# Folding the first batch of a spectral mixture-of-experts kernel: 4-KB loads, sums and differences before the transform, quartered matmuls

## The chip, the cores and the metric

The kernel runs on one core of one Trainium2 chip. The metric is the device time of one execution in microseconds; the time of a kernel is the median of its runs. The engines are TensorE (PE in the profile; PEld is its weight load), VectorE (DVE), ScalarE (ACT), GpSimd (POOL) and SyncE (SP), which here issues the transfers.

## The reference, cut to what matters

Eight batches of 3072 x 256 go through a real Fourier transform along the sequence, a complex 256 x 256 mix with bias and soft threshold, and the inverse transform; a soft mixture of experts and a gated block with layer norm follow.

```python
X = np.fft.rfft(x, axis=1)                       # x: 8 x 3072 x 256
Yr = Xr @ w_r - Xi @ w_i + b_r
Yi = Xr @ w_i + Xi @ w_r + b_i
Yr = np.sign(Yr) * np.maximum(np.abs(Yr) - 0.01, 0)      # Yi likewise
y = np.fft.irfft(Yr + 1j * Yi, n=3072, axis=1)
# soft MoE over the 24576 rows of y: softmax over rows, experts on 32 slots, softmax over slots
# then h = x @ w_in;  solu = h * softmax(h);  layer norm;  @ w_out
```

## The kernel before

The transform of 3072 points is split as 96 x 32. Stage 1 is a transform over the 96 rows that lie 32 apart (index n1), for each of the 32 offsets n2; stage 2 combines the 32. The result of stage 1 goes through a DRAM buffer `ad`, because the two stages need different axes on the partitions. `load_ap` reads `ad` back, `stage2` transforms, `mix` multiplies with the weights (each fp32 operand split into a high and a low part, so three products), and so on. Phase 1 does this for the 8 batches in 12 steps each; phase 2, from about 620 us on, does the expert and the gated block.

Stage 1 exists in two forms. For batches 1 to 7 (`load_x`, `xfold`, `xdiff`, `stage1`, `a_fold`) it is folded: rows n1 and n1 + 48 are added and subtracted first, by POOL, and the sums and differences go through two 48 x 48 transforms. A unit holds four n2: two in partitions 0 to 47, two in partitions 64 to 111. Its four matmuls use a constant `fold` of 128 x 128, each a quarter of the array with 48 rows and up to 64 columns, and it stores 48 partitions at a time. Units 8 to 63 are spread over the steps of the main loop by `s1_next`.

Batch 0 has a form of its own (`load_x0`, `stage1_first`, `a_out`): 16 pieces of two n2 each. A piece is loaded with 2-KB rows into 96 partitions, goes through one 96 x 96 matmul with the constant `dft` (the profile shows two instructions for one fp32 product), is copied from PSUM by ACT and stored to `ad` by SP. All 16 loads are issued first, into buffers of the pool `s_p`. Nothing else can be done before the first blocks of `ad` can be read, except the preparation of the mix weights (`weights`, on DVE).

Order is written out by hand. Each engine executes its instructions in program order. `after(n, f)` puts a step off by n ticks, and `tick()` runs what is due. SP issues all transfers in program order: a transfer that must wait holds up those behind it. Behind the 16 pieces come `load_ap(0,0,0)`, a part of the constant `d2_sb`, `fold`, `load_x(8)` (the first load of batch 1), `load_ap(0,0,1)`, the bias and `load_x(9)`, then the main loop. Pools `ap_p`, `xt_p`, `y_p`, `st_p` for the main loop are opened at the beginning of phase 1.

## Time and profile before

| | us |
|---|---|
| median of 3 runs | 1340.09 |
| lowest, highest | 1338.70, 1341.55 |
| the profiled execution | 1339.27 |
| its span | 1337.2 |

| engine | busy us | share of the span |
|---|---|---|
| PE | 1265.9 | 95% |
| PEld | 1113.8 | 83% |
| DVE | 1143.4 | 86% |
| POOL | 1020.3 | 76% |
| ACT | 987.7 | 74% |

The page has one profiled execution. Busy shares are averages over the whole span; the edit is at its beginning, so the views by stretch of time and the chain of waits are read in what follows. Times of rows count from the first instruction. In a row of the timeline stand start, duration, engine, line, operation, output<-input by the program's names, shape and count; a bracket at the end is the idle time before it and what ended it. Rows with a count above one are merged, and their duration is from the first start to the last end.

### The profile page before, as it was taken

How to read it: one execution, taken by the hardware profiler on the slowest of the kernel's cores; microseconds unless marked ns; L12 is line 12 of the kernel's file. 1: busy time of each engine (PE TensorE's matmuls, PEld its weight loads, DVE VectorE, ACT ScalarE, POOL GpSimd, SP SyncE). 2: the span in 40 equal slices, each digit the busy share in tenths (PEclk: the TensorE clock that was granted, in tenths of full speed). 3: DMA queues.
4: the chain of work that ended last, by engine and by line, in shares of the span. 5: the costliest groups of instructions: out<-in, count | busy, mean ns of one | idle time of the engine just before them, and what ended most of it. 6: DMA issues, size and time to landing. Idle time of an engine off the chain costs nothing.

```text
span 1337.2 us, 30847 instructions
## 1 busy us (share of the span) xinstructions
PE 1265.9 (95%) x10980; PEld 1113.8 (83%) x10980; DVE 1143.4 (86%) x1562; ACT 987.7 (74%) x1830; POOL 1020.3 (76%) x1116
## 2 busy tenths in 40 slices
PE   5989999999999999998599999999999999999998
PEld 2867878786867778875399999999999999999998
DVE  1868898887897979765898999999999999999993
ACT  3445556555555555544598999999999999999995
POOL 0868696877767674442299999998999989999996
PEclk8999999999999999999699999999999999999999
DMA  9987474654639273339567777777777777777763
GB/s 267 277 219 189 118 206 126 173 160 125 192 82 247 72 206 138 112 115 364 123 165 195 190 214 193 190 189 184 201 195 196 181 190 199 189 201 176 196 169 109
DMA packets 181337, 241.77 MB, mean 181 GB/s; under 512 B 21984, under 2 KB 137056, under 8 KB 181184
## 3 DMA queue, kind: packets, MB, share of 16 engines
q1 hardware_dynamic: 180736, 238.62, 66.3%
q8 instruction: 87, 1.43, 0.5%
q10 hardware_dynamic: 448, 1.18, 0.2%
q14 instruction: 66, 0.54, 0.1%
HBM read 92.00 MB, written 59.11 MB: 113 GB/s over the span
## 4 chain that ended last, share of the span: by engine, by line
PE 69%; DVE 10%; DMA 7%; POOL 5%; issue 4%; ACT 3%; SPq 2%; DVEq 0%; POOLq 0%; ACTq 0%
PE po L89 33%; PE pb L89 8%; PE pm L89 6%; PE xps L89 5%; PE hps L89 5%; PE s L89 4%; PE pa L89 3%; POOL ul L1177 2%; DMA xc<-in_x_dram 2%; DVE u L1082 2%; PE sps L92 2%; PE hps L92 1%; DVE st L1067 1%; DVE tb L1105 1%; DMA ad<-asb 1%
## 5 line engine op out<-in xcount | busy, mean ns | idle before, releaser
L1177 POOL TENSOR_TENSOR ul<-t,uh 128x512 fp32r<-128x512 f32 x338 | 433.4, 1299 | 37.5 <-ACT uh L1163 35.1
L89 PEld LDWEIGHTS po<-gw,uh 128*128 128x128 f32 x2736 | 350.5, 190 | 14.0
L89 PE MATMUL po<-gw,uh 128*128 128x256 f32 x2736 | 356.9, 282 | 0.0
L1067 DVE TENSOR_REDUCE st<-hps 128x1 f32<-128x1024 f32 x192 | 229.2, 1194 | 14.0 <-PE hps L89 13.9
L89 PE MATMUL po<-gw,ul 128*128 128x256 f32 x1620 | 230.8, 285 | 6.8 <-POOL ul L1177 6.6
L1082 DVE SCALAR_TENSOR_TENSOR u<-hps,e 128x1024 f32<-128x1024 f32 x192 | 232.2, 1209 | 0.5 <-ACT e L1074 0.3
L1074 ACT ACTIVATE e<-hps,st 128x1024 f32<-128x1024 f32 x192 | 215.5, 1123 | 16.8 <-DVE st L1067 16.7
L1187 ACT ACTIVATE sq<-u,st 128x1024 f32<-128x1024 f32 x192 | 223.0, 1161 | 0.3 <-DVE u L1082 0.3
L1105 DVE STREAM_TRANSPOSE tb<-u 128x1024 f32<-128x1024 f32 x169 | 210.5, 1246 | 7.0 <-DMA t<-tb 1.2
L89 PEld LDWEIGHTS po<-gw,ul 128*128 128x128 f32 x1620 | 207.5, 189 | 9.4 <-POOL ul L1177 8.4
L347 POOL TENSOR_TENSOR s<-yb,s 128x512 f32<-128x512 f32 x95 | 124.6, 1312 | 113.4 <-DVE s L346 109.8
L89 PEld LDWEIGHTS xps<-d_sb,apt 128*128 128x128 f32 x768 | 95.0, 194 | 59.7 <-issue 35.3
L1163 ACT ACTIVATE uh<-t 128x768 fp32r<-128x768 f32 x169 | 143.6, 850 | 0.9 <-DMA t<-tb 0.9
L89 PE MATMUL xps<-d_sb,apt 128*128 128x128 f32 x768 | 111.0, 288 | 13.1 <-DMA apt<-ad 10.2
L89 PE MATMUL hps<-gst,ct 128*128 128x512 f32 x338 | 107.7, 401 | 13.9 <-DVE u L1082 12.5
L250 ACT ACTIVATE asb<-s 128x1024 f32<-128x1024 f32 x56 | 57.6, 1029 | 82.9 <-PE s L89 71.4
L223 POOL TENSOR_TENSOR x<-xc 112x512 f32<-112x512 f32 x56 | 75.4, 1347 | 42.8 <-DMA xc<-in_x_dram 39.8
L307 POOL TENSOR_TENSOR sl<-xsum,sh 128x256 fp32r<-128x256 f32 x93 | 76.3, 821 | 37.1 <-ACT sh L306 36.9
L291 DVE TENSOR_TENSOR xsum<-xps,xi 128x256 f32<-128x256 f32 x96 | 39.9, 415 | 67.3 <-ACT xh L290 48.0
L1238 ACT ACTIVATE osb<-po,st 128x256 f32<-128x256 f32 x192 | 80.3, 476 | 11.4 <-PE po L89 11.4
L1164 POOL CAST uh<-t 128x256 fp32r<-128x256 f32 x169 | 68.4, 405 | 24.6 <-DMA t<-tb 24.6
L227 POOL TENSOR_TENSOR x<-xc 112x512 f32<-112x512 f32 x56 | 79.1, 1413 | 0.0
(210 smaller groups left out, 2373.5 us busy)
## 6 DMA issues: line engine op xcount, KB each, us to landing
t<-tb SPq DMA_DIRECT2D x676, 128.0 KB, 2.8
xc<-in_x_dram SPq DMA_DIRECT2D x128, 192.0 KB, 4.1
apt<-ad SPq DMA_DIRECT2D x96, 256.0 KB, 4.1
out_dram<-osb SPq DMA_DIRECT2D x47, 512.0 KB, 3.7
ad<-asb SPq DMA_DIRECT2D x112, 192.0 KB, 3.9
ct<-c_dram SPq DMA_DIRECT2D x96, 128.0 KB, 4.0
wt<-in_moe_w_dram SPq DMA_DIRECT2D x21, 512.0 KB, 9.6
ws<-in_moe_w_dram SPq DMA_DIRECT2D x22, 256.0 KB, 5.4
```

The costliest lines, as they stand in the source:

```text
L89: PE.matmul(out=out, lhsT=lhsT, rhs=rhs, start=start, stop=stop)
L227: POOL.tensor_tensor(out=z[0:112, 1], in0=t[:, 0], in1=t[:, 1], op=ALU.subtract)
L307: (POOL if (b, t) > (0, 2) else DVE).tensor_tensor(out=sl, in0=sm_, in1=sh.bitcast(F32), op=ALU.subtract)
L347: POOL.tensor_tensor(out=s, in0=y, in1=s, op=ALU.subtract)
L1067: DVE.tensor_reduce(out=st[:, 0, k:k + 1], in_=hps[i], op=ALU.min, axis=AX.X)
L1074: ACT.activation(out=e, in_=hps[i], func=AF.Exp, bias=st[:, 0, k:k + 1], scale=-1.0, accum_out=st[:, 1, k:k + 1])
L1082: DVE.scalar_tensor_tensor(out=u, in0=hps[i] if turned(i) else hps.pop(i), scalar=1.0, in1=et.pop(i), op0=ALU.mult, op1=ALU.mult, accum_ou ...
L1105: DVE.transpose(out=t, in_=ut[i])
L1163: ACT.activation(out=w[:, 0:HA], in_=v[:, 0:HA], func=AF.Copy)
L1177: POOL.tensor_tensor(out=ul[:, z, :].rearrange("p c (a j) -> p c a j", a=4), in0=v, in1=w.bitcast(F32), op=ALU.subtract)
L1187: ACT.activation(out=sq, in_=ut.pop(i), func=AF.Square, bias=st[:, 2, k:k + 1], scale=-float(DFF), accum_out=st[:, 3, k:k + 1])
L1238: ACT.activation(out=o[:, k], in_=pot.pop(i), func=AF.Copy, scale=stt[j][:, 4, k:k + 1])
```

## The change

Batch 0 is folded as well. Its 8 units take two buffers' halves each: four buffers `xt[v]` of 128 x 2 x 4 x 256, each loaded by two transfers with 4-KB rows into 48 partitions (64 to 111 first, then 0 to 47). Partitions 32 to 63 of the buffers are filled with zero before, by DVE and POOL in turn. The buffers lie in a pool `x0_p` that is closed before the pools of the main loop are opened, so these take its place. A unit's sum is made by DVE, its difference by DVE (even units) or POOL (odd units). The matmuls go to two PSUM banks, are copied by two ACT instructions, and two transfers store the unit. `fold` is loaded first of all, `dft` is gone. Six matmuls on `ones` (`warm(6)`) stand before the first unit and 34 behind `weights()`, ahead of stage 2 on TensorE. `load_x(8)` is issued before `load_ap(0,0,0)`. The order of the constants in the early loads is kept, at other unit numbers.

```diff
-        ap_p = right("ap_p", 2)
-        xt_p = right("xt_p", 2)
-        y_p = right("y_p", 2)
-        st_p = right("st_p", 5)
...
-        def load_x0(ch):
-            t = s_p.tile([96, 2, D], F32, name="xc0", tag="s")
-            SP.dma_start(out=t, in_=x[0].rearrange("(a n) d -> a n d", n=32)[:, 2 * ch:2 * ch + 2, :])
-            xt[ch] = t
+        x0_open = ExitStack()
+        x0_p = x0_open.enter_context(tc.tile_pool(name="x0_p", bufs=1, side="right"))
+
+        def load_x0(v, r):
+            rows = x[0].rearrange("(h a n) d -> a h n d", h=2, n=32)
+            SP.dma_start(out=xt[v][64 * r:64 * r + 48], in_=rows[:, :, 8 * v + 4 * r:8 * v + 4 * r + 4, :])
...
-        def stage1_first(ch):
-            if ch == 0:
+        def stage1_first(u):
+            v, w = divmod(u, 2)
+            if u == 0:
                 ad[0] = dram2.tile([32, 4, 24, D], F32, name="ad", tag="ad")
-            dst = s_p.tile([96, 2, D], F32, name="a0", tag="s")
-            after(LAG["a_out"], a_out, 0, 2 * ch, 2, dst)
-            pool, tag = ((ps1, "s1"), (pst, "sps"), (psm, "pm"))[ch % 3]
-            ps = pool.tile([96, 2, D], F32, name="s1", tag=tag)
-            mm(ps, dft, xt.pop(ch))
-            ACT.activation(out=dst, in_=ps, func=AF.Copy)
+            t = xt[v][0:112, :, w::2, :]
+            z = xc[u % 2] if u % 4 > 1 else wa_p.tile([128, 2, 2, D], F32, name="x1", tag="x1")
+            DVE.tensor_tensor(out=z[0:112, 0], in0=t[:, 0], in1=t[:, 1], op=ALU.add)
+            (POOL if w else DVE).tensor_tensor(out=z[0:112, 1], in0=t[:, 0], in1=t[:, 1], op=ALU.subtract)
...
+            unit(ps, z)
+            if u % 4 > 1:
+                dst = wa_p.tile([128, 2, 2, D], F32, name="a0", tag="asb")
+            else:
+                dst = sm_p.tile([128, 2, 2, D], F32, name="a0", tag=("sa", "sb", "sc")[u // 4 + u % 4])
+            for r in range(2):
+                ACT.activation(out=dst[:, r], in_=ps[r], func=AF.Copy)
+            after(LAG["a_out"], a_first, v, w, dst)
+
+        def a_first(v, w, t):
+            for c in range(2):
+                o = ad[0][:, 2 * c:2 * c + 2].rearrange("(v m w) k g d -> v w (k g) m d", v=4, w=2)
+                SP.dma_start(out=o[v, w], in_=t[64 * c:64 * c + 48])
+
+        def unit(ps, z):
+            for k in range(2):
+                for r in range(2):
+                    c = (k + r) % 2
+                    mm(ps[r][64 * c:64 * c + 64], fold[64 * r:64 * r + 48, 64 * c:64 * c + 64], z[64 * r:64 * r + 48, c])
...
-        for ch in range(16):
-            load_x0(ch)
+        def warm(n):
+            ps = psy.tile([128, 128], F32, name="warm", tag="pa")
+            for _ in range(n):
+                mm(ps, ones, ones)
+
+        load_const(fold, c_fold)
         POOL.memset(ones, 1.0)
+        for v in range(4):
+            xt[v] = x0_p.tile([128, 2, 4, D], F32, name=f"x0{v}")
+            (DVE, POOL)[v % 2].memset(xt[v][32:64], 0.0)
+        warm(6)
+        for v in range(4):
+            for r in (1, 0):
+                load_x0(v, r)
...
-        for pr in range(16):
-            stage1_first(pr)
...
+        for u in range(8):
+            stage1_first(u)
...
         tick()
+        x0_open.close()
+        ap_p = right("ap_p", 2)
...
         weights()
+        warm(34)
+        load_x(8)
         load_ap(0, 0, 0)
         load_const(d2_sb[:, 2:8, :], c_d2[:, 2:8, :])
-        load_const(fold, c_fold)
-        load_x(8)
         load_ap(0, 0, 1)
```

## Rows read from the trace of the kernel before

**Rows 1.** The page's first line.
```profile
span 1337.2 us, 30847 instructions
```

**Rows 2.** Chain of waits, first 60 us: start us, length us, what.
```profile
4.06 16.98 PE s L89 x32
21.06 0.60 ACT a L238
...
22.12 3.09 DMA ad<-a
...
25.33 2.83 DMA apt<-ad
...
28.30 2.15 PE xps L89 x8
...
32.63 2.05 PE xps L89 x8
34.68 3.43 PE pb L89 x18
```

**Rows 3.** Busy time by window: window, length, engines (instructions), PEclk, DMA share, GB/s.
```profile
3.50:13.00 9.50, 8.94 (x14) 3.26 (x15) 0.00 (x0) 3.49 (x6) 0.00 (x0) 1.00 1.04 263
...
25.00:28.00 3.00, 0.00 (x0) 0.00 (x0) 0.00 (x0) 0.00 (x0) 0.00 (x0) 0.50 0.53 145
...
29.90:31.30 1.40, 0.54 (x3) 0.24 (x2) 0.00 (x0) 0.83 (x2) 0.00 (x0) 0.50 1.09 231
...
100.00:120.00 20.00, 20.00 (x173) 15.62 (x172) 17.21 (x22) 11.19 (x22) 18.25 (x16) 1.00 0.71 190
606.00:612.00 6.00, 5.19 (x88) 4.55 (x88) 3.36 (x9) 3.23 (x7) 0.00 (x0) 1.00 1.03 414
```

**Rows 4.** First four and last load of batch 0, first `load_ap`: issue, landing.
```profile
L205 SPq DMA_DIRECT2D xc<-in_x_dram x4: 405/423/426, 1.2 to 2.6; - x4
...
DMA to landing us min/median/max: 2.7/3.5/4.3
...
L205 SPq DMA_DIRECT2D xc<-in_x_dram x1: 312/312/312, 10.0 to 10.0; - x1
...
DMA to landing us min/median/max: 5.3/5.3/5.3
...
L266 SPq DMA_DIRECT2D apt<-ad x2: 343/384/426, 25.3 to 25.7; - x2
...
DMA to landing us min/median/max: 2.8/3.1/3.4
```

**Rows 5.** Timeline of DVE and POOL in the first 45 us.
```profile
1.39 1.84 POOL L787 MEMSET xc<- 128x1024 f32 x2
19.89 0.68 DVE L792 TENSOR_TENSOR wk<-wc 128x512 f32<-128x512 f32 x1
33.02 0.43 DVE L307 TENSOR_TENSOR sl<-xsum,sh 128x256 fp32r<-128x256 f32 x1
39.38 1.29 POOL L227 TENSOR_TENSOR x<-xc 112x512 f32<-112x512 f32 x1
42.33 1.46 POOL L227 TENSOR_TENSOR x<-xc 112x512 f32<-112x512 f32 x1
42.58 1.49 DVE L307 TENSOR_TENSOR sl<-xsum,sh 128x256 fp32r<-128x256 f32 x1
```

**Rows 6.** Timeline of TensorE and its weight loads.
```profile
34.27 0.97 PEld L89 LDWEIGHTS pb<-wc_h,xh 128*128 128x128 f32 x4
38.52 0.98 PEld L89 LDWEIGHTS xps<-d_sb,apt 128*128 128x128 f32 x8
39.42 0.54 PEld L89 LDWEIGHTS pb<-wc_h,xh 128*128 128x128 f32 x4
41.72 1.09 PE L89 MATMUL s<-x,fold 48*64 48x512 f32 x8
...
611.68 1.52 PEld L89 LDWEIGHTS idle<-ones 128*128 128x128 f32 x12
```

More of the change, by code (lines that the diff above doesn't have):

```diff
@@ L245, in stage1 @@
             ps = ps1.tile([128, 2, 2, D], F32, name="s1", tag="s1")
-            for k in range(2):
-                for r in range(2):
-                    c = (k + r) % 2
-                    mm(ps[64 * c:64 * c + 64, r], fold[64 * r:64 * r + 48, 64 * c:64 * c + 64], z[64 * r:64 * r + 48, c])
+            unit([ps[:, 0], ps[:, 1]], z)
             ACT.activation(out=dst, in_=ps.rearrange("p r n d -> p (r n) d"), func=AF.Copy)
@@ L720, in sums, with load_const @@
                 DVE.tensor_scalar(out=mexp, in0=mexp, scalar1=srun, scalar2=None, op0=ALU.mult)
+        def load_const(o, i):
+            SP.dma_start(out=o, in_=i)
         dec_ops = []
@@ L785, in phase1 @@
         POOL.memset(zx, 0.0)
-        for t in xc:
-            POOL.memset(t, 0.0)
         def weights():
```

28 lines of the change are left out of this document (15 added, 13 removed).

## The prediction

> **What bounds the kernel now.** The span comes first [rows 1]: it is 1337.2 us, in an execution timed at 1339.27 us, so 2.1 us lie around it. The median of the three runs is 1340.09 us. I subtract changes in the stretch that the edit touches and quote the result against the median; the profiled execution is 0.8 us below it.
>
> Next I read the chain of waits for the first 60 us [rows 2], because the edit touches nothing later. The reader is to see a row of handovers with one engine at a time. TensorE runs 32 stage-1 matmuls without a break from 4.06 to 21.04. One ScalarE copy of 0.60 follows, then the last store of stage 1 (issued 22.12, 3.09 to landing), then the first load of the intermediate (issued 25.33, 2.83 to landing), and at 28.30 stage 2 begins. Whatever moves 25.33, and whatever runs faster between 28.30 and the steady state, moves the end.
>
> [...] And from 100 to 120 us TensorE is busy 20.00 of 20 us: from there a head start is carried along by the bound engine. A gain at 28 to 40 us should therefore reach the end nearly whole.
>
> **The change, part by part.**
>
> *Loads.* Sixteen loads of 192 KB (2-KB rows into 96 partitions) become eight of 384 KB (4-KB rows into 48 partitions, upper half first). The bytes stay 3.15 MB. Before, the first four loads are 786 KB, the last of them issued at 2.6 and landed 4.3 later [rows 4]: 6.8 us. The last load lands at 10.0 + 5.3 = 15.3. In between the queues are full at 263 GB/s [rows 3]. The first pair of new loads is these same 786 KB. What 4-KB rows into 48 partitions cost is not in the trace, so I bound it. The rows at 29.9 to 31.3 us cover mostly a load of x into 48 partitions: 231 GB/s. Contiguous 4-KB rows into 128 partitions at 606 to 612 us: 414 GB/s. I take the 263 of the same data in the same place and let the first pair land at 6.8, with bounds 5.4 (786 KB at 414 instead of 263 saves 1.1 us, and I allow 0.3 for the shorter backlog) and 7.5 (at 231 it costs 0.4, and the fills below may add).
>
> [...]
>
> *Zero fill.* The fills of partitions 32 to 63 precede the second load of each pair. POOL fills 1024 elements in 0.92 us [rows 5], so 2048 in 1.84; DVE has no such row, and four times its 0.68 for 512 elements, 2.7, bounds it from above. SP stands in front of them in order, with the later loads behind it; but the first load of each pair is issued before the fill is waited for and needs 1.5 us of the queues at 263 GB/s. That is the cover. At 2.7 about 0.7 us would show, once, in the landing of the first pair.
>
> *Sums and differences.* New on the path: per pair three DVE operations and one POOL operation on 112 x 512 elements. DVE's comparable one took 0.68 [rows 5], POOL's 1.29. They don't run side by side: the DVE subtraction of 128 x 256 took 0.43 alone at 33.02, and 1.49 at 42.58 with a POOL subtraction in 42.33 to 43.79, ending 0.3 after it. So I add them: 3 x 0.66 + 1.26 = 3.25 us for a pair (spacing instead of duration). Pairs of loads arrive every 2.8 us ((15.3 - 6.8) / 3), slightly faster, so this is a chain that never drains: four pairs from 6.8 end at 19.8. If nothing collided, it would end about 2 us after the last load: 17.3. Queued behind it on DVE is the preparation of the mix weights, whose second instruction started at 19.89 before; it moves by less than 1 us and the mix that waits for it begins above 30, so it costs nothing.
>
> *Matmuls.* A folded unit took 1.09 us at the upper level [rows 6], eight take 8.7; 32 full ones took 17. The new ones aren't continuous at first, and I expect the first two or three units at the lower rate (before, the first 14 matmuls took 0.64 us each, the 18 behind them 0.45 [rows 2, 3]). TensorE has room for that, 3.25 us a pair. The last unit ends 1.1 to 1.45 after the chain: about 21.1, against 21.04 before. The path through TensorE is not shorter; the arithmetic it loses had been paid by waiting anyway.
>
> *Copies and stores.* ScalarE now makes two copies of 0.6 for the last unit, 0.6 more than before, and the second of its two stores is issued 0.4 behind the first. The last landing becomes 21.1 + 1.2 + 0.4 + 3.0 = 25.7 against 25.21. The queues themselves would allow 25.1: after the last load of x the same stores and weights need 25.2 - 15.3 = 9.9 us in both. Copies of units 4, 6 and 7 reuse buffers whose stores may land just in time; at most 0.6 us. So the load of the intermediate starts at about 25.8, **0.45 us later than before**; bounds are -1.5 and +1.5.
>
> *Moved load of batch 1 and the fold constant.* load_x(8) now goes ahead of load_ap: two issues of 0.4 us on SP and 1.5 us on the queues, both inside the 3 us in which the last store is landing. Without that cover they would cost up to 1.5. Gone from behind load_ap are these 384 KB and the 64 KB of the fold constant: d2, the second intermediate block and the bias land earlier by up to 1.9 us. That is needed, since the next step wants them earlier.
>
> *Warm matmuls.* 34 pairs of 128 x 128. The same product elsewhere took 1.52 us for 12 [rows 6], 0.12 each, so 68 x 0.12 = 8.2 us: from 21.1 to 29.3. The intermediate lands at 28.6, its second half 1.0 later, as before (25.7 + 3.4 against 28.16 [rows 4]). So they end beside the landing, and cost about 0.2. What they bring: stage 2 and the first mix run at the upper level. At the lower one the first group of eight took 2.15 and the second 2.05 [rows 2]; the same eight at 38.52 give way to the next after 0.90 [rows 6]. Walked through, from the landing: first group done after 1.75 instead of 2.28 (the second half of the block lands only 1.0 behind), the second group starts at 3.94 instead of 4.47 (ScalarE and DVE between them unchanged), the mix follows 0.90 instead of 1.67 later, and its 24 matmuls take 0.117 each, as at 39.42, where the first dozen took about 0.21, as at 34.27. The next stage-2 group starts 7.65 after landing instead of 10.36: **2.7 us won**. DVE, next in line there, gets its inputs 2.8 earlier as well.
>
> **Sum:** 2.7 - 0.45 - 0.15 = 2.1 us. 1339.27 becomes 1337.2 in an execution like the profiled one, and the median 1340.09 becomes **1338.0 us**.
>
> **The rivals.**
>
> *Faster loads.* If 4-KB rows run near 414 GB/s, the first pair lands at 5.4 and the chain of sums ends at 18.4: 1.4 more won, 1336.6. If sums and differences collide less as well, up to 3 more: 1335. For it: the contiguous rows. Against: the same destination partitions held 263. I put it at 1336.0.
>
> [...] Loads into half of the partitions hold 231 GB/s throughout, and less where one half waits for the other. At 231 they need 13.6 us instead of 12, the last pair lands 1.7 later, the last sums end 0.45 later: 1338.5; 1 us more of it gives 1339.5, still no difference that shows. [...]
>
> *The warm matmuls come late or run at the lower level* (the slower end). They stand in TensorE's order ahead of stage 2. If the units, in pieces, don't raise the clock, eight of them take 2 x 1.09 us each from about 9.4, to 27, and 68 warm ones at twice 0.12 take 16: the end is 43, 14.5 us after 28.30, less the 2.7. If the clock rises 6 us into the warm ones, they end at 32.7, 4.4 after 28.30, and the kernel is 1.7 us slower: 1341.8, and up from there. It decides from an end of the warm matmuls at about 31 us. Against it: before, 6 us of matmuls in a row were enough to run at the upper rate.
>
> *It doesn't arrive.* The transfers behind 40 us may be too full to let through what TensorE has won, and the gain ends as waiting for data: 1340.
>
> **How the numbers follow.** Forecast 0.60 (1336.4 to 1339.6; 1338.0), faster loads 0.20, ports 0.08, late warm matmuls 0.09, not arriving 0.03. About 0.2%, 2.7 us, is what a measurement of this kernel can tell from no change, so the line is 1337.4. It cuts the forecast's own range, 0.22 on the faster side and 0.38 on the other. Faster: 0.22 + 0.19 = 0.41. Same: 0.38 + 0.01 + 0.07 + 0.03 = 0.49. Slower: 0.10. The range 1335.0 to 1341.0 leaves out the best of the fast loads and most of the late warm matmuls.
>
> **What would show it.** In the trace of the changed kernel: first pair landed near 6.8; DVE and POOL stretched against each other until 19.8; the last unit near 21; load_ap at 25.3 to 26.3; the warm matmuls ending within 1 us of its landing; a granted clock of 1.00 from 25 to 40 us, and the first mix's end 2 us earlier. The prediction fails if load_ap is issued before 24 or after 27, if the clock is 0.50 behind the units, or if the head start at 40 us isn't found at 100 us.

## The result and the profile after

The changed kernel takes 1347.43 us (1342.40 to 1349.64, six runs) against 1338.55 us of the kernel before in the same runs. By these medians it is slower by 8.9 us, a quotient of 1.0066; the ratio estimated from the runs, as in the table below, is 1.0087 with a 95% interval of 1.0061 to 1.0112. So it is slower, clear of noise; the forecast was 1338.0 us, with a range of 1335.0 to 1341.0. The profiled execution took 1349.3 us, and its span is 10.3 us longer than that of [rows 1]:

```profile
span 1347.5 us, 31080 instructions
```

The sums by window of the changed kernel, as [rows 3]: window, its length, busy time of PE, PEld, DVE, ACT and POOL, granted clock, DMA share, GB/s.

```profile
3.50:13.00 9.50, 3.69 (x12) 1.21 (x14) 4.57 (x4) 0.00 (x0) 3.39 (x5) 1.00 1.03 164
...
29.40:37.60 8.20, 8.20 (x69) 8.13 (x68) 1.49 (x5) 1.08 (x2) 0.00 (x0) 1.00 0.79 215
37.60:40.50 2.90, 1.40 (x10) 1.04 (x8) 0.00 (x0) 0.00 (x0) 1.26 (x1) 1.00 0.95 322
40.50:47.50 7.00, 4.70 (x23) 4.61 (x22) 3.56 (x13) 2.58 (x6) 0.00 (x0) 0.52 0.94 243
```

The first line is the finding. The DMA share is 1.03 against 1.04 before, so the queues are just as full, but they move 164 GB/s instead of 263. The last line is the second finding: behind the warm matmuls the clock falls after all, to 0.52 in the mean from 40.5 to 47.5 us.

A third is hidden by the column of the granted clock. It prints 1.00 also where the trace has no record of the clock yet: the first record, a rise to 1.00, stands at 10.1 us in the kernel before and at 30.5 us in the changed kernel. The matmuls themselves show the level ahead of it. The groups below are the folded matmuls of the changed kernel between 9.5 and 29.3 us, and the same form in the kernel before between 39.5 and 66 us (count, then busy time and mean ns of one):

```profile
L88 PE MATMUL s<-x,fold 48*64 48x512 f32 x32 | 10.7, 1071 | 5.8 <-DVE x L232 5.8
```
```profile
L89 PE MATMUL s<-x,fold 48*64 48x512 f32 x40 | 5.4, 615 | 0.0
```

The other 32 of the changed kernel took 1070. So all eight units ran at the lower level, and it rose only 1.2 us into the warm matmuls. In the kernel before, the 96 x 96 matmuls took 1069 ns each up to 10.1 us and 612 behind it.

Issues and landings of the changed kernel, as [rows 4]: the first two loads, the last two, and the first block read back.

```profile
L202 SPq DMA_DIRECT2D x<-in_x_dram x2: 315/363/411, 1.2 to 3.0; - x2
...
DMA to landing us min/median/max: 5.2/5.5/5.8
...
L202 SPq DMA_DIRECT2D x<-in_x_dram x2: 357/394/431, 5.5 to 6.0; - x2
...
DMA to landing us min/median/max: 15.5/16.3/17.1
...
L281 SPq DMA_DIRECT2D apt<-ad x2: 351/387/423, 35.8 to 36.2; - x2
...
DMA to landing us min/median/max: 2.9/3.3/3.6
```

The first pair has landed at 3.0 + 5.8 = 8.8 us, the last load at 6.0 + 17.1 = 23.1, where 6.8 and 15.3 were forecast. The eight landings are 2.4 us apart, and 384 KB in 2.4 us are 163 GB/s. load_ap is issued at 35.84 us, 10.5 us later than before.

The timeline of DVE and POOL, as [rows 5]; a bracket is the idle time before the row and what ended it.

```profile
8.96 0.69 DVE L232 TENSOR_TENSOR x<-x 112x512 f32<-112x512 f32 x1 [3.85 <-DMA x<-in_x_dram]
9.57 1.75 DVE L233 TENSOR_TENSOR x<-x 112x512 f32<-112x512 f32 x1
11.25 0.68 DVE L232 TENSOR_TENSOR x<-x 112x512 f32<-112x512 f32 x1
13.87 0.69 DVE L232 TENSOR_TENSOR xc<-x 112x512 f32<-112x512 f32 x1 [1.94 <-DMA x<-in_x_dram]
...
9.00 1.77 POOL L233 TENSOR_TENSOR x<-x 112x512 f32<-112x512 f32 x1 [3.83 <-DMA x<-in_x_dram]
```

A pair takes 2.97 us (8.96 to 11.93) and then DVE waits 1.94 for the next load: the loads set the pace, not the sums.

The timeline of ScalarE and SP behind the loads:

```profile
25.52 2.06 ACT L247 ACTIVATE a<-s 128x512 f32<-128x512 f32 x4 [4.37 <-DMA ad<-a]
...
21.05 7.82 SPq L253 DMA_DIRECT2D ad<-a  x8
...
30.45 2.56 SPq L253 DMA_DIRECT2D ad<-a  x4
...
35.84 0.83 SPq L281 DMA_DIRECT2D apt<-ad  x2
```

The copy at 25.52 has waited 4.37 us for a store that had to land out of the same buffer, behind the loads. SP is at eight stores for 7.82 us, its waits for their copies included.

The weight loads of TensorE, as [rows 6]:

```profile
29.33 8.20 PEld L88 LDWEIGHTS warm<-ones 128*128 128x128 f32 x68 [1.61 <-issue]
39.00 0.52 PEld L88 LDWEIGHTS xps<-d_sb,apt 128*128 128x128 f32 x4 [1.47 <-issue]
...
42.89 1.78 PEld L88 LDWEIGHTS xps<-d_sb,apt 128*128 128x128 f32 x8 [2.47 <-issue]
44.55 0.97 PEld L88 LDWEIGHTS pb<-wc_h,xh 128*128 128x128 f32 x4
...
48.74 0.98 PEld L88 LDWEIGHTS xps<-d_sb,apt 128*128 128x128 f32 x8
```

The warm matmuls take the 8.2 us that were forecast, but TensorE then waits 1.3 us in front of the first group of stage 2 and 2.3 us in front of the second, and the level falls at 40.7 us, as the second wait begins. The mix spends 0.97 us on four weight loads, as at 34.27 before, and the third group starts at 48.74, 10.2 us behind the 38.52 of before. So in these two executions the whole loss of 10.3 us is there at 35.84 us and is carried to the end.

It splits in two. The last load of x lands 7.7 us late (23.1 against 15.4). From there to the landing of the last store it takes 12.6 us (to 35.70) instead of 9.8 (15.38 to 25.21): 2.8 us more. Together they are the 10.5. The two are not independent, as a run with punctual loads will show. The experiments take these two, and the clock behind 28 us, one by one; no run changes the clock of the units alone, whose last matmul ends 3.1 us behind the last sum (26.27 to 29.41), where it is 1.4 us in e10 (20.48 to 21.87) with its last units at the upper level.

### The profile page after: what moved, and what is told of

Read it like the earlier page. It is cut to its first block, busy times and chain, and to the rows that moved or that the text cites. A ratio compares the mean times of both kernels' runs of the same rounds, so it can differ in the third digit from the quotient of the medians.

```text
span 1347.5 us, 31080 instructions
## 1 busy us (share of the span) xinstructions
PE 1279.9 (95%) x11092; PEld 1124.0 (83%) x11092; DVE 1165.2 (86%) x1576; ACT 986.1 (73%) x1830; POOL 1027.9 (76%) x1120
## 4 chain that ended last, share of the span: by engine, by line
PE 61%; POOL 11%; DVE 9%; issue 6%; DMA 5%; SPq 3%; ACT 2%; POOLq 0%; DVEq 0%; ACTq 0%
PE po L88 33%; PE pb L88 6%; PE hps L88 5%; PE pm L88 5%; PE xps L88 4%; DMA xc<-in_x_dram 3%; POOL ul L1204 3%; PE pa L88 2%; PE s L88 2%; POOL x L219 2%; PE hps L91 1%; POOL x L223 1%; SPq L1136 1%; PE sps L91 1%; POOL s L362 1%
## 5 line engine op out<-in xcount | busy, mean ns | idle before, releaser
L1101 ACT ACTIVATE e<-hps,st 128x1024 f32<-128x1024 f32 x192 | 215.0, 1120 | 17.1 <-DVE st L1094 17.1
L322 POOL TENSOR_TENSOR sl<-xsum,sh 128x256 fp32r<-128x256 f32 x93 | 76.1, 818 | 35.1 <-ACT sh L321 34.9
```

The costliest lines, as they stand in the source:

```text
L1101: ACT.activation(out=e, in_=hps[i], func=AF.Exp, bias=st[:, 0, k:k + 1], scale=-1.0, accum_out=st[:, 1, k:k + 1])
```

## The experiments

One table for the loads and stores; the columns are landing times in us from the traces. "Between" is the time from the last load of x to the last store of stage 1. The ratios are against the kernel before in runs beside each. The kernels e6, e7, e10, e11, e13, e17 and e18 time the stage and do not compute the transform: they load other rows, and e13, e17 and e18 also store other data.

| kernel | last load | last store | between | load_ap issued | ratio (95%) |
|---|---|---|---|---|---|
| before | 15.38 | 25.21 | 9.8 | 25.33 | 1 |
| changed | 23.11 | 35.70 | 12.6 | 35.84 | 1.0087 (1.0061 to 1.0112) |
| e3 before, 4-KB rows | 14.82 | 24.80 | 10.0 | 24.99 | 1.0016 (0.9998 to 1.0035) |
| e6 source flat | 21.60 | 34.37 | 12.8 | 34.51 | 1347.8 us, one run |
| e7 128 partitions | 15.45 | 30.84 | 15.4 | 30.98 | 1.0053 (1.0032 to 1.0073) |
| e2 2-KB rows | 20.04 | 32.76 | 12.7 | 32.90 | 1.0106 (1.0073 to 1.0138) |
| e8 halves in turn | 18.52 | 31.48 | 13.0 | 31.63 | 1.0068 (1.0046 to 1.0089) |
| e1 two queues | 23.23 | 39.28 | 16.1 | 39.42 | 1.0130 (1.0093 to 1.0166) |
| e10 = e7 + own buffers | 16.36 | 31.33 | 15.0 | 31.48 | 1.0059 (1.0037 to 1.0080) |
| e11 = e10 + two issuers | 15.55 | 29.28 | 13.7 | 29.43 | 1.0054 (1.0035 to 1.0073) |
| e13 = e10 + 96-part. stores | 15.58 | 28.97 | 13.4 | 29.12 | 1.0035 (1.0020 to 1.0051) |
| e17 = e13 + two issuers | 16.17 | 28.49 | 12.3 | 28.64 | 1.0042 (1.0025 to 1.0059) |
| e18 = e13 - sums | 16.49 | 27.94 | 11.5 | 28.09 | 1.0026 (1.0008 to 1.0044) |
| e14 before, half stores | 15.08 | 27.17 | 12.1 | 27.36 | 1.0009 (0.9993 to 1.0026) |
| e12 all together | 19.28 | 33.30 | 14.0 | 33.52 | 1.0103 (1.0079 to 1.0127) |

Each landing is read from one execution. Loads that are the same in e7, e10, e11, e13, e17 and e18 landed between 15.45 and 16.49, and "between" was 9.86 in e15 and 10.75 in e16, two kernels below whose stage 1 and order of transfers are the same. So differences under about 1 us in these columns show nothing. Nor does load_ap give the time one to one: e2 has it 2.9 us earlier than the changed kernel and is no faster, and e11, with load_ap 4.1 us later than before, loses 6.5 us in the medians. These runs don't show where the rest is lost.

### What makes the loads slow

The suspects were the rows of 4 KB, the source (rows that lie 32 KB apart, in two pieces) and the destination (48 partitions). The first run puts 4-KB rows into the kernel before.

```diff
-            t = s_p.tile([96, 2, D], F32, name="xc0", tag="s")
-            SP.dma_start(out=t, in_=x[0].rearrange("(a n) d -> a n d", n=32)[:, 2 * ch:2 * ch + 2, :])
+            t = x0_p.tile([96, 4, D], F32, name=f"x0{ch}")
+            SP.dma_start(out=t, in_=x[0].rearrange("(a n) d -> a n d", n=32)[:, 4 * ch:4 * ch + 4, :])
...
```

> The kernel before with 4-KB rows: its sixteen loads of 192 KB into 96 partitions become eight of 384 KB into the same 96 partitions (buffers in the place of the later block buffers, matmuls and copies as before). Theory 'destination': 263 GB/s as before, 1.49 us per load, the last landing at 15.3 +- 0.5 us, and the time within 1.5 us of the kernel before (the first matmul starts up to 0.8 us later, because twice as much must land for it). Theory 'rows': 163 GB/s, 2.4 us per load, the last landing at 22 to 23 and the time 5 to 8 us above the kernel before.

The window 4.5 to 12.5 us of this kernel, in the columns of the windows above:

```profile
4.50:12.50 8.00, 7.19 (x11) 2.62 (x12) 0.00 (x0) 2.53 (x5) 0.00 (x0) 1.00 1.03 275
```

275 GB/s: 4-KB rows into 96 partitions are no slower than 2-KB rows. The length of the rows is out as the main cause.

The next run keeps the destination and makes the source contiguous.

```diff
-            rows = x[0].rearrange("(h a n) d -> a h n d", h=2, n=32)
-            SP.dma_start(out=xt[v][64 * r:64 * r + 48], in_=rows[:, :, 8 * v + 4 * r:8 * v + 4 * r + 4, :])
+            o = 768 * v + 384 * r
+            rows = x[0][o:o + 384].rearrange("(h a n) d -> a h n d", h=2, n=4)
+            SP.dma_start(out=xt[v][64 * r:64 * r + 48], in_=rows)
```

> The changed kernel, its eight loads to the same 48 partitions in the same 4-KB rows, but each from one contiguous stretch of 384 KB of x instead of rows that lie 32 KB apart; the data are other rows than the transform wants, so batch 0 is computed from wrong rows. Theory of the destination: nothing changes, 163 GB/s, landings 2.4 us apart, the last at 23. Rival, the source: rows that lie 32 KB apart were the slow part, then 263 GB/s or more, landings at most 1.5 us apart, the last at 15.5 or earlier.

The same window of this kernel:

```profile
4.50:12.50 8.00, 3.24 (x10) 1.11 (x13) 3.58 (x4) 0.00 (x0) 2.40 (x5) 1.00 1.02 182
```

182 GB/s in this window, landings 2.2 us apart. Even the small gain over 163 can't be put down to the source: in e4 below, whose loads are those of the changed kernel unaltered, the same window shows 178 GB/s, and the landings are 2.23 us apart.

```profile
4.50:12.50 8.00, 3.25 (x10) 1.10 (x13) 3.57 (x4) 0.00 (x0) 2.39 (x5) 1.00 1.03 178
```

So one and the same load into 48 partitions ran at 163 GB/s in one execution and at 178 in another, and the source doesn't show as a cause. The counterpart keeps the source's pitch and changes the destination.

```diff
+            rows = x.rearrange("b s d -> (b s) d")[0:4096].rearrange("(a n) d -> a n d", n=32)
+            SP.dma_start(out=xt[v][:, r], in_=rows[:, 8 * v + 4 * r:8 * v + 4 * r + 4, :])
```

> The changed kernel, its eight loads in 4-KB rows that lie 32 KB apart as there, but into all 128 partitions, one half of the buffer's free axis each: 512 KB a load instead of 384, 4.2 MB instead of 3.1; the sums are made of wrong rows of x. Theory of the destination: about 414 GB/s, 1.27 us a load, first pair landed at 6.3, last at about 13.8 in spite of a third more bytes. The rest of the prediction then shows what it is worth with loads that are not late: sums and differences 4 x 2.97 us from 6.3 to 18.2 or, where loads wait for the fills, 1 later; load_ap issued between 24 and 26, the warm matmuls end beside its landing, granted clock 1.00 to 40 us, time 1.5 to 4 us below before, ratio 0.997 to 0.999. Rival, the source: 163 GB/s or less, 3.2 us a load, the last landing at 29, ratio 1.012 or more.

The same window of this kernel:

```profile
4.50:12.50 8.00, 3.83 (x13) 1.34 (x16) 5.19 (x6) 0.13 (x1) 3.91 (x6) 1.00 1.00 402
```

402 GB/s; 512 KB land every 1.28 us. The same 4-KB rows at the same pitch give 163 to 178, 275 and 402 GB/s into 48, 96 and 128 partitions. The destination is the cause, and that is shown from both sides.

So that the destination sets the rate is shown; what in the destination does it, no run here shows.

Then three ways to have both halves of the partitions written at once. Smaller loads in the old order (two for 64 to 111, two for 0 to 47), the same loads in turn, and the second half issued by ScalarE.

```diff
+            for h in range(2):
+                n = 8 * v + 4 * r + 2 * h
+                SP.dma_start(out=xt[v][64 * r:64 * r + 48, :, 2 * h:2 * h + 2], in_=rows[:, :, n:n + 2, :])
```

> The changed kernel with 2-KB rows: each load of 384 KB into 48 partitions becomes two of 192 KB into the same 48 partitions. Theory 'destination': nothing changes, 1.2 us per load of 192 KB, the last landing at 22 to 23.5 us and the time within 2 us of the changed kernel. Theory 'rows': the rate is that of the kernel before again, 263 GB/s or 0.75 us per load; the last lands at 14 to 15.5 and the time falls by 5 to 9 us.

The same window of this kernel:

```profile
4.50:12.50 8.00, 3.74 (x13) 1.35 (x16) 3.97 (x5) 0.03 (x1) 2.80 (x6) 0.67 1.08 192
```

192 GB/s, landings 1.0 us apart, and no gain in time. The rate lies between what the two theories expected; that it comes from overlap where one half follows the other is a guess that this run doesn't test.

```diff
+            for k in (1, 0):
+                n = 8 * v + 4 * k + 2 * (1 - r)
+                SP.dma_start(out=xt[v][64 * k:64 * k + 48, :, 2 * (1 - r):2 * (1 - r) + 2], in_=rows[:, :, n:n + 2, :])
```

> The changed kernel, its loads halved to sixteen of 2-KB rows (as in the experiment with 2-KB rows), but the halves of the partitions taken in turn: 64 to 111, 0 to 47, 64 to 111, 0 to 47 for each buffer. Same bytes, same rows, same number of transfers as there. Theory of the destination: transfers that follow one another now write to different halves and go on together where one was the limit for itself; between the 191 GB/s of that experiment and twice 163, I take 230 GB/s: last landing at 17, load_ap issued at about 28 to 30, ratio 1.002 to 1.006. Rival, the order of the halves is nothing and only the number of rows counts: 191 GB/s, last landing 20.0, load_ap at 33, ratio 1.010.

The same window of this kernel:

```profile
4.50:12.50 8.00, 3.79 (x13) 1.34 (x16) 4.52 (x5) 0.09 (x1) 3.35 (x6) 0.71 1.06 228
```

228 GB/s, as the theory of the destination had it: the order of the halves alone is worth a fifth over e2. But the last load lands at 18.52 instead of the 17 expected, 3.1 us later than before, and load_ap at 31.63 instead of 28 to 30.

```diff
-            SP.dma_start(out=xt[v][64 * r:64 * r + 48], in_=...)
+            (SP if r else ACT).dma_start(out=xt[v][64 * r:64 * r + 48], in_=...)
```

> The changed kernel, with the second half of each pair of loads (partitions 0 to 47) issued by ACT instead of SP, so that both halves can be in flight side by side. In the changed kernel the eight loads land one after the other, 2.4 us apart: 384 KB each, 163 GB/s, where the kernel before held 263. Theory 'destination': a transfer that writes only 48 partitions is limited by the part of the memory that it reaches, and the two halves reach different parts. Then two at a time run at 260 to 330 GB/s, the first pair lands near 5.5 us (8.8 now), the last near 13 (23.1 now), load_ap is issued at 25 to 27 (35.8 now), and the time falls by 8 to 11 us, to 1337 to 1340. Theory 'rows': 4-KB rows that lie 32 KB apart in DRAM are read slowly whatever they are written to. Then the pairs land no earlier than now, the last near 23, and the time stays within 2 us of the changed kernel.

The two halves were mostly not in flight together: SP's four loads landed first (6.56 to 15.46 us), ScalarE's behind them (15.87 to 23.23), and the last landing is where it was. Both moved only from 10 to 14 us, at 160 GB/s in the first half of that and at 234 in the second. So this run doesn't decide between its two theories; as an improvement it fails, since every pair of halves is complete later.

### What is late when the loads are not

The run with 128 partitions was meant as a check of the rest of the prediction: its last load lands at 15.45 us, as forecast (its first pair at 7.8 instead of 6.8), and its sums end at 19.5. Yet load_ap is issued at 30.98 instead of 25.8. So punctual loads bring back 4.9 of the 10.5 us and not 7.7, and in the time 1.0053 against 1.0087, with intervals that overlap. The loads were not the only fault. First suspect: the copies, which wait about 2 us for stores to land.

```diff
-            z = xc[u % 2] if u % 4 > 1 else wa_p.tile([128, 2, 2, D], F32, name="x1", tag="x1")
+            z = [s_p.tile([128, 2, D], F32, name=f"x1{c}", tag="s") for c in range(2)]
...
+            if u < 2:
+                dst = xc[u]
+            elif u < 6:
+                dst = wa_p.tile([128, 2, 2, D], F32, name="a0", tag="x1" if u < 4 else "asb")
+            else:
+                dst = sm_p.tile([128, 2, 2, D], F32, name="a0", tag=("sa", "sb")[u - 6])
```

> The kernel with loads into 128 partitions (loads land as the prediction wanted, and yet load_ap is issued at 30.98 us), in which each of the eight units has a copy buffer of its own, so that no copy waits for a store (the sums and differences go to buffers of the pool of small blocks instead). As there, the sums are made of wrong rows. Theory of the copies: ScalarE's waits of 2.0 us (for stores to land) are gone, the last copy ends at 22.4 instead of 24.42 and load_ap is issued 2 us earlier, at 29; ratio 1.004. Rival, the stores: SP issues them back to back from 17.6 to 28 us anyway, 0.45 to 1.5 us each, so that the copies only wait longer in front of SP; load_ap at 30.5 to 31, ratio unchanged at 1.005.

SP's timeline of this kernel:

```profile
18.43 6.52 SPq L255 DMA_DIRECT2D ad<-a  x8
...
25.81 2.61 SPq L255 DMA_DIRECT2D ad<-a  x4
```

The last copy ends at 23.14 although the loads landed 0.9 later, and nothing is won: the rival holds. SP is at its stores up to 28.4 us; "between" falls by 0.4 us, which is within the scatter. So the stores were looked at. In the changed kernel each takes 48 partitions; before, each took 96. The next two expectations speak of a theory of the ports; what they test is only whether the rate of a store goes with the number of its partitions, as that of the loads did. What lies behind that, ports or anything else, no run here shows.

```diff
-                o = ad[0][:, 2 * c:2 * c + 2].rearrange("(v m w) k g d -> v w (k g) m d", v=4, w=2)
-                SP.dma_start(out=o[v, w], in_=t[64 * c:64 * c + 48])
+                n = 8 * v + 4 * w + 2 * c
+                SP.dma_start(out=ad[0][n:n + 2].rearrange("n k g d -> (k g) n d"), in_=t[0:96, c])
```

> The kernel with loads into 128 partitions and own copy buffers (last copy 23.14, last store landed 31.33, load_ap issued 31.48, ratio 1.006), whose sixteen stores of 192 KB take 96 partitions and two n2 each instead of 48 partitions and four n2; same bytes, same 1-KB pieces, same issuer. What is stored is not what the transform wants, as its input isn't either. Theory of the ports, now for the stores: with 96 partitions the stores run at 380 GB/s as in before, SP is not held up, the last store lands at 26 to 27, load_ap is issued at 26 to 27.5, ratio 1.000 to 1.002. Rival, SP: its issues are long for another reason and the stores stay at 250 GB/s, load_ap at 31, ratio 1.005. Rival, the units: copies that end at 23.1 set it, with the same result as the first theory but a store queue that runs empty from 20 us on.

And the reverse, 48-partition stores in the kernel before. There two pieces share a copy buffer (not in the cut below), so that a store waits for both; its second store takes partitions 48 to 95.

```diff
+                o = ad[0][n:n + 4].rearrange("n k g d -> (k g) n d")
+                SP.dma_start(out=o[48 * c:48 * c + 48], in_=t[48 * c:48 * c + 48].rearrange("p r n d -> p (r n) d"))
```

> The kernel before, loads, matmuls and copies as they were (copies of two pieces share a buffer), but the two stores of two pieces take 48 partitions and four n2 each (0 to 47, 48 to 95) instead of 96 partitions and two n2. Sixteen stores of 192 KB as before. Theory of the ports: the stores slow down by themselves, from 381 to about 260 to 300 GB/s, 3 to 4 us more between the last load and the last landing (9.8 in before), load_ap at 28 to 29, ratio 1.002 to 1.003. Rival: the number of partitions of a store is nothing, its rate stays at 380 and load_ap comes at 25.3 to 26.3 (two pieces have to be waited for), ratio 1.000.

The window 17 to 23 us, in which stores are nearly all that moves, first of before, then of e14, e10 and e13:

```profile
17.00:23.00 6.00, 4.02 (x10) 1.30 (x8) 3.61 (x6) 3.33 (x6) 0.00 (x0) 1.00 1.08 369
```
```profile
17.00:23.00 6.00, 3.51 (x9) 1.06 (x7) 4.57 (x8) 2.97 (x5) 0.00 (x0) 0.99 0.95 282
```
```profile
17.00:23.00 6.00, 5.40 (x45) 2.65 (x41) 4.69 (x6) 5.43 (x12) 1.13 (x1) 1.00 0.92 270
```
```profile
17.00:23.00 6.00, 5.91 (x52) 3.29 (x43) 5.45 (x8) 5.11 (x10) 0.27 (x1) 1.00 1.01 318
```

Half stores cut before from 369 to 282 GB/s, as their theory said, and move its load_ap from 25.33 to 27.36, less than the 28 to 29 expected; up to 1 us of that may be the wait for the second piece, which its expectation allowed for. Whole stores bring e10 from 270 to 318, and "between" down by 1.6 us. In the time e14 is at 1.0009, within its interval of no change, and the intervals of e10 and e13 overlap, so these 1.6 to 2.3 us are shown in single traces alone. And e13 came only half the expected way: the rate did not return to 380. Two more runs ask for the rest. Two issuers:

```diff
-                SP.dma_start(out=ad[0][n:n + 2]...
+                (ACT if c else SP).dma_start(out=ad[0][n:n + 2]...
```

> The kernel with loads into 128 partitions, own copy buffers and stores from 96 partitions (last copy 22.28, last store issued 25.20 and landed 28.97, load_ap 29.12, ratio 1.0035), whose second store of each unit is issued by ScalarE. There SP spends 0.4 to 1.25 us on each of its issues. Theory of SP's issues: two issuers take half each, the stores follow the copies, the last lands at 26, load_ap at 26 to 26.5, ratio 1.000 to 1.001. Rival, the transfers: the issues are only long because the engines of the queues are busy, the last store lands between 28 and 29 as before, ratio 1.003.

With 96 partitions "between" is 1.1 us shorter with the second issuer, and the time is no better, at a ratio of 1.0042; with 48 partitions it had been 1.2 us:

> As the run with own copy buffers, and the second store of each unit (partitions 64 to 111) is issued by ScalarE instead of SP, so that stores of the two halves are issued side by side. Theory of the stores: one half at a time, they ran at 200 to 270 GB/s where before held 380; with both halves in flight they run above 300 GB/s, the last lands at about 26 and load_ap is issued at 26 to 27, ratio 1.000 to 1.001. Rival, the copies: no further gain over own buffers, load_ap at 29, ratio 1.004. Rival: two queues are served one behind the other, as for the loads, and nothing is won.

There the last store lands at 29.28 instead of 26. Both differences are near the scatter of about 1 us, so that two issuers help at all is not shown. And the kernel of e13 without sums and differences, so that the units follow the loads directly:

```diff
-            z = [s_p.tile([128, 2, D], F32, name=f"x1{c}", tag="s") for c in range(2)]
-            DVE.tensor_tensor(out=z[0][0:112], in0=t[:, 0], in1=t[:, 1], op=ALU.add)
-            (POOL if w else DVE).tensor_tensor(out=z[1][0:112], in0=t[:, 0], in1=t[:, 1], op=ALU.subtract)
+            z = [t[:, c] for c in range(2)]
```

> As the kernel with stores from 96 partitions, all stores by SP, but without the sums and differences: the units take the loaded halves as they are (what batch 0 computes is then no folded transform at all). Theory of the sums: the chain of DVE and POOL, 3 us a pair, sets when stores can be issued; without it the last unit ends 2 us behind the last load, at 17.6, the copies at 19, the queues stay full from 16 us on and the last store lands at 15.5 + 9.9 = 25.4 as in before, load_ap at 25.5, ratio 1.000. Rival, SP and the transfers: stores at 290 GB/s whenever they are ready, the last at 28, load_ap at 28 or later, ratio 1.002 to 1.003.

The window 17 to 23 us of this kernel:

```profile
17.00:23.00 6.00, 6.00 (x56) 4.87 (x49) 2.88 (x4) 2.13 (x5) 0.00 (x0) 1.00 1.09 377
```

Now the queues are full with 377 GB/s, the copies end at 19.84 instead of 22.28, and "between" falls by another 1.9 us, to 11.5. So the chain of sums can cost about that much by holding stores back: in e13 the DMA share is 0.84 from 16 to 17 us and 0.92 from 18 to 19, in e18 it is 1.08 or more from 16 to 20. But it isn't isolated. Without the sums the units also start earlier and the clock rises at 12.5 us instead of 16.4, and in the time the intervals of e13 and e18 overlap. About 1.6 us against before remain, with the last load 1.1 us later; no run here explains these.

### What the clock is worth

Warm matmuls in the kernel before, with its fast loads: once 30 ahead of stage 2.

```diff
+        ps = psy.tile([128, 128], F32, name="warm", tag="pa")
+        for _ in range(30):
+            mm(ps, ones, ones)
         load_ap(0, 0, 0)
```

> The kernel before, with 30 matmuls on ones (60 of 0.12 us, 7.2 us) between the last unit of stage 1 (ends 21.04) and stage 2 (28.30); nothing else. Theory of the clock: what the prediction counted as 2.7 us is there, whatever the loads do: granted clock 1.00 from 21 to 40 us, the second group of stage 2 and the first mix at the upper level, the third group of stage 2 starts 2.7 us earlier than the 38.52 of before, and the time is 2.7 us lower, a ratio of 0.998. Rival, the gain does not arrive: 2.7 us earlier at 40 us and nothing at the end, ratio 1.000. Rival, the warm matmuls end too early and the pause in front of the second group (28.5 to 32.6 us in before) loses the level again, as in the changed kernel at 40.6: 0.50 from some point between 29 and 33 us, ratio 1.000.

The ratio is 1.0001 (0.9981 to 1.0022). Windows and weight loads of this kernel:

```profile
28.00:32.00 4.00, 1.39 (x8) 1.04 (x8) 1.01 (x4) 0.87 (x2) 0.00 (x0) 0.83 1.00 266
32.00:38.00 6.00, 5.75 (x29) 5.78 (x30) 3.14 (x14) 1.70 (x4) 1.27 (x1) 0.54 1.07 267
```
```profile
32.22 1.78 PEld L89 LDWEIGHTS xps<-d_sb,apt 128*128 128x128 f32 x8 [2.36 <-issue]
33.88 0.97 PEld L89 LDWEIGHTS pb<-wc_h,xh 128*128 128x128 f32 x4
```

The second rival holds: the weight loads pause for 2.36 us in front of the second group, the granted clock is 0.54 on average from 32 to 38 us, and nothing is won. In the changed kernel it fell at the beginning of the same pause. There, more warm matmuls reach further:

```diff
-        warm(34)
+        warm(42)
```

> The changed kernel with 42 warm matmuls instead of 34 ahead of stage 2, so that they end near 39.5 us and not at 37.6, with load_ap landing at 38.8 to 39.9. In the changed kernel's profile the granted clock falls to 0.50 at 40.6 us for 6.8 us. Theory 'clock': the pause of TensorE behind the warm matmuls is what lets it fall, and the executions at 1342 to 1345 are those in which it didn't; with 42 it stays at 1.00 and the median falls by 1.5 to 3 us, with less spread. Rival: the spread has another cause and the 0.50 costs nothing on the path; then the median stays within 1 us and the spread stays 5 us or more.

The window behind the warm matmuls and the first group of stage 2, and the weight loads of the second group:

```profile
42.00:48.00 6.00, 4.95 (x44) 4.79 (x43) 3.72 (x8) 2.16 (x5) 0.24 (x1) 1.00 0.98 264
```
```profile
41.52 0.97 PEld L88 LDWEIGHTS xps<-d_sb,apt 128*128 128x128 f32 x8 [2.47 <-issue]
```

The level is kept, although the pause in front of the second group is as long as before, 2.47 us. What is gone is the gap of 1.3 us between the warm matmuls and the first group. So that pause alone doesn't lose the level. The third group of stage 2 comes at 45.2 instead of 48.7; load_ap was 1.1 us earlier in that execution. But the fifth group comes at 57.4 against 57.8, and the ratio of 1.0078 (1.0048 to 1.0107) can't be told from 1.0087. With the pause filled in the kernel before:

```diff
         stage2(0, 0)
         stage2s(0, 0)
+        ps = psy.tile([128, 128], F32, name="warm", tag="pa")
+        for _ in range(9):
+            mm(ps, ones, ones)
```

> The kernel before with the 30 matmuls on ones ahead of stage 2 and 9 more (18 of 0.12 us, 2.2 us) in the pause between the first and the second group of stage 2, where the granted clock fell back to 0.50 with the 30 alone (TensorE idle from 29.9 to 32.2 us). Theory of the pause: with it filled the level stays at 1.00 from 21 to 40 us, the second group takes 0.9 and the first mix is at the upper level, the third group starts at 35.8 to 36.2 instead of 38.34 (before: 38.52), and the gain of 2.5 us reaches the end: ratio 0.998. Rival, not arriving: the third group 2.5 us earlier, ratio 1.000, because transfers or waits behind 40 us take it back; then the head start is gone by 60 us. Rival: the level falls all the same, ratio 1.000.

The weight loads of TensorE in this kernel:

```profile
31.18 0.97 PEld L89 LDWEIGHTS xps<-d_sb,apt 128*128 128x128 f32 x8 [0.35 <-issue]
32.06 0.54 PEld L89 LDWEIGHTS pb<-wc_h,xh 128*128 128x128 f32 x4
...
34.88 0.97 PEld L89 LDWEIGHTS xps<-d_sb,apt 128*128 128x128 f32 x8
```

The upper level all through, and the third group at 34.88, 3.6 us earlier than before (0.8 of it an earlier load_ap). Yet the ratio is 0.9999 (0.9985 to 1.0013): 2.7 us would be 0.998, just outside the interval. The fifth group starts at 47.0 against 48.1. The chain of waits shows where the first part went:

```profile
28.70 7.08 DMA bias<-in_b_i_dram
...
36.72 0.70 DVE yb L335
```

The result of the first mix can't be read before the bias has landed, and that was queued behind the blocks of the intermediate. So the bias, the constant d2 and fold were moved ahead of load_ap, without and with the warm matmuls.

```diff
+        load_const(d2_sb[:, 2:8, :], c_d2[:, 2:8, :])
+        for k, z in enumerate((b_r, b_i)):
+            load_const(bias[:, k, :], z.rearrange("(o e) -> o e", o=1).to_broadcast([128, D]))
+        load_const(fold, c_fold)
         load_ap(0, 0, 0)
```

> The kernel before, with d2_sb[2:8], the two loads of the bias and the fold constant issued ahead of load_ap(0,0,0), while SP waits for the last store to land (22.5 to 25.3 us, queues empty from 24.5 to 27). No warm matmuls. Theory: with the level at 0.50 the first mix ends at 38.1, after the bias has landed at 36.4 in any case; nothing to win, third group of stage 2 at 38.6, ratio 1.000. Rival: less is queued behind 28 us, the second block lands earlier and later groups of stage 2 wait less: the fourth and fifth group 1 us earlier, ratio 0.999.

> The kernel before with that order of the loads and with the 30 and 9 warm matmuls. With the warm matmuls alone the third group of stage 2 came 3.6 us earlier, but the chain went through the landing of the bias at 35.8, and the ratio was 1.000. Theory of the bias: it lands at 28 now, the first mix is read at 34.5 instead of 36.7, the fifth group of stage 2 starts 2.5 to 3 us earlier than the 48.1 of before and the end follows: ratio 0.998. Rival: something else behind it (POOL's sums for the next batch, the second block of the intermediate) takes the head start back by 60 us: ratio 1.000.

Neither was faster: 1.0013 (0.9995 to 1.0032) and 1.0012 (0.9997 to 1.0026). The chain of waits of e16, where it passes through the load of the first block:

```profile
25.79 6.75 DMA apt<-ad
```

The bias lands at 29.7 now, and the block of the intermediate takes 6.75 us instead of 3.4: it lands at 32.5, the third group comes at 40.4, and the fifth at 51.0, 2.9 us later than before. The clock fell as well, to 0.50 from 29.2 to 36 us. The wait was moved, not removed. That the bias alone takes back the head start is therefore not shown: in e9 the bias was late, and in e15 and e16 the block was.

Nor would the bias have been the last wait. The chain of the kernel before, read on from 51 us, has no TensorE in it from 51.1 to 93.3 us:

```profile
56.88 8.43 DMA ft_sb<-in_c_ft_dram
...
65.37 7.47 DMA xc<-in_x_dram
...
72.85 7.10 DMA xc<-in_x_dram
...
88.51 4.77 DMA apt<-ad
```

From 60 to 100 us TensorE is busy for 35.1 of 40 us. So a head start of TensorE at 40 us has to pass 40 us in which transfers and POOL set the pace, before the stretch from 100 us in which it is busy all the time. In e9, one conversion by ScalarE behind stage 2 that stands at 109.4 us in the kernel before comes 1.4 us earlier; of the 3.6 us at the third group that is what is left in this execution, and 0.8 of it is the earlier load_ap. That transfers and POOL absorb the rest is read from the chain and not tested by a run.

Last, what seemed to help, put together in the changed kernel (loads in turn, own buffers, stores by SP and ScalarE, nine warm matmuls in the pause):

> The changed kernel with what helped so far, computing what it should: loads in turn to the two halves (2-KB rows, last landing 18.5), own copy buffers, stores issued by SP and ScalarE, and 9 more warm matmuls in the pause between the first two groups of stage 2. If the loads were the whole cause: load_ap at 31, as with the alternating loads alone, ratio 1.006. If copies and stores carry 4 us of it, as the loads into 128 partitions suggest: load_ap at 27 to 28, 2 us behind before, the level kept at 1.00 up to 40 us gives 2.5 back: ratio 0.999 to 1.001. Rival: ratio below 0.998, a version faster than both.

1.0103: no better than the change itself. Its last load landed at 19.28, as the last of the loads was issued only at 14.6 us (11.5 in e8), for a reason that these runs don't show, and its stores were no faster (14.0 us between). No version here is faster than the kernel before.

## Why the prediction was wrong, point by point

**The rate of the loads** is the step that failed first. The prediction took "the 263 of the same data in the same place" with 231 GB/s as the lower bound; 163 was measured. The nearest row had been chosen by the data and not by the number of partitions. The row of 231 GB/s was said to "cover mostly" such a load; it covers two, into the two halves, issued 0.4 us apart (27.20 and 27.62), and loads to the halves in turn ran at 228 in e8. It was no bound for one half alone. Instead of 6.8 and 15.3 us the landings are 8.8 and 23.1. That is 7.7 us of the 10.5 by the landings, of which 4.9 come back when the loads are punctual (e7).

**The rival of the loads into half of the partitions** ("ports" in the chances, 0.08) named the right cause, the destination, and the wrong size: it took 231 GB/s, and 163 to 178 was measured. That ports bind no run shows; what the runs show is the rate by partitions, 163 to 178 GB/s into 48, 275 into 96 and 402 into 128.

**The sums and differences** were right: 2.97 us for a pair against 3.25, DVE's difference going from 0.68 to 1.75 and POOL's from 1.29 to 1.77 where they run side by side. They didn't set the pace because the loads did. Where the loads were fast, their chain ended at 19.5 (19.8 forecast).

**The units** were expected at the lower rate for "the first two or three" only. All eight ran at it, 1.07 us a matmul against 0.62, and the last unit ended 3.1 us behind the chain of sums instead of 1.1 to 1.45. What this costs at load_ap no run isolates. The first condition of the rival of late warm matmuls came true with it ("If the units, in pieces, don't raise the clock"); but the warm matmuls raised it within 1.2 us, so they were not late. (The 32.7 us of that rival don't follow from its units ending at 27: 6 us at 0.24 and the rest at 0.12 end near 38.)

**The stores** are the second step that failed, hidden by the first. That "after the last load of x the same stores and weights need 25.2 - 15.3 = 9.9 us in both" is wrong: they need 12.6 in the changed kernel and 15.4 where the loads are on time. By single traces, half stores cost 1.6 to 2.3 us of that (e13, e14), the chain of sums in front of them up to 1.9 (e18), and the rest stays open. The forecast that copies of units 4, 6 and 7 wait "at most 0.6 us" missed the 4.37 us at 25.52; but without these waits nothing changed clear of the scatter (e10).

**The warm matmuls** took the 8.2 us forecast and ended at 37.5, ahead of the landing at 38.8. Not foreseen was that TensorE would wait 1.3 us in front of the first group of stage 2 and 2.3 us behind it ([rows 2] has the second wait already, 2.2 us at 30.45), and that the level would fall there. With the first wait filled it stayed (e4), and so it did in the kernel before with the second one filled (e9). The 2.7 us were then priced rightly as far as the third group (2.8 in e9, without the earlier load_ap) and wrongly as a gain of the whole: "it doesn't arrive", with a chance of 0.03, is what happened where the level was kept. The argument looked at TensorE from 100 us on; but between 28 and 48 us it waits for landings (the bias in e9, the first block in e16), and from 51 to 93 us the chain runs through transfers and POOL, which had gained nothing.

**Signs that were named.** "The prediction fails if load_ap is issued before 24 or after 27": 35.84. And "if the clock is 0.50 behind the units": the printed 1.00 is no reading up to 30.5 us, the matmuls ran at the lower level to the last unit, and the clock was 0.52 again from 40.5 us. There was no head start at 40 us. The zero fills took 1.76 us on DVE, below the 2.7 that bounded them, and cost nothing that shows.

## What to carry to other kernels

The rate of a transfer went here with the partitions it touched, on either end: loads moved 163 to 178, 275 and 402 GB/s into 48, 96 and 128, and stores 270 to 282 from 48 and 318 to 377 from 96. Before a load or store is reshaped to 48 partitions, find a row of that very shape, alone in the queue, and take the lowest as the bound; the same load still varied from 163 to 178 GB/s here. This stage, whose transfers filled the queues before (a DMA share of 1.04 from 3.5 to 13 us, 1.08 from 17 to 23), didn't get shorter by halving its matmuls: with punctual loads load_ap still came at 30.98 us instead of 25.33 (e7). A serial step put between load and store can leave the queue less than full: with the sums the share was 0.84 from 16 to 17 us (e13), without them 1.08 or more (e18), though the sums were not the only difference. A head start on TensorE is worth what the next landing allows (3.6 us at the third group of e9, and a ratio of 0.9999): follow the chain on, past the one wait that is removed, to where TensorE sets the pace. And check a granted clock of 1.00 at the start of a trace against the mean time of one matmul (1071 ns under a printed 1.00 here, 615 for the same form in the kernel before).

## What the runs showed of the hardware

The same 4-KB rows moved 163 to 178 GB/s into 48 partitions, 275 into 96 and 402 into 128, each with a DMA share of 1.00 to 1.03: a full share told nothing of the rate here. Loads into the two halves of the partitions, in turn in one queue, reached 228. From 17 to 23 us stores from 48 partitions ran at 270 to 282 GB/s, stores from 96 at 318 (e13), 369 (before) and 377 (e18). Two issuers did not share evenly: up to 10 us only the loads of SP moved, and the last of them landed (15.46) ahead of the first of ScalarE (15.87); both moved only in a stretch of 4 us, from 10 to 14. TensorE read as busy all the time from 15 to 29.4 us with 48 x 64 matmuls of 1.07 us each, and the level did not rise; 1.2 us of 128 x 128 matmuls behind them it did, at 30.5 us. With 7 us of matmuls ahead, gaps of 0.75 and 0.22 us around the first group and a pause of 2.2 us behind it, the granted clock fell to 0.50 at 30.7 us (e5); the same pause behind a group that followed the warm matmuls without a gap kept 1.00 (e4), and so did 18 matmuls in the pause (e9).
